# Chunked attention feeding a squared-ReLU FFN on one core: x of two groups transposed by DMA, and a block that begins in halves

## The chip, the core and the metric

The kernel runs on one core of one Trainium2 chip. The metric is the device time in microseconds (us), median of the runs. "PE" below is TensorE, "DVE" VectorE, "ACT" ScalarE, "POOL" GpSimd and "SP" SyncE, which here does nothing but issue DMAs.

## The reference

Attention over chunks of 64 tokens, for batch 8, 8 heads, 576 tokens and head size 64, and then an FFN without a gate:

```python
scores = scale * np.matmul(q_c, k_c.transpose(0, 1, 2, 4, 3))      # within a chunk of 64
attn = exp(scores - max); attn = attn / (attn.sum(-1) + 1e-09)
out = np.matmul(attn, v_c)
x = out.transpose(0, 2, 1, 3).reshape(B * S, H * D)                # 4608 x 512
h = np.maximum(x @ w_in, 0.0)                                      # 512 -> 2048
return h * h @ w_out                                               # 2048 -> 512
```

## The kernel before, in words

The 4608 tokens are 18 groups of 256 tokens; two groups make a block of 512, so there are nine blocks, numbered 0 to 8. For each group the kernel loads q, k and v, casts q and k to bf16 (`C`, lines L271 and L274; on POOL up to group 7, on ACT from group 8), transposes both (`TD`, L280, a DMA transpose on the SP queue from group 4), multiplies them (`SC`, scores, L303) and takes the exponential (L314, ACT), multiplies with v (`AV`, values, L330), divides by the sum (`rec` L337 and `x` L338, DVE), and transposes x (`XT`). In `XT`, groups below `FIRST_DMA_X` go through PE into PSUM and an ACT copy (L357, L361); the others use one DMA transpose (L351).

The FFN of a block has two phases. `ffn_in` goes over 16 d_ff tiles; each has four matmuls over d_model (L414) into one PSUM bank, a ReLU on ACT (`rl`, L430), and a square on DVE or ACT (`gT`, L442 or L440). `ffn_out` is a Strassen-like scheme (from block 1 on) with seven products, in this order: n (a22), m (a11), n (d5), m (d2), n (d1), m (d6), n (d7). Each product is 16 matmuls (L500) in two pieces. The differences d1 to d7 of quarters of gT are made on DVE (L395). The products named n share one PSUM bank, and those named m another; each sum is read out of its bank between two products, and the next product into that bank waits for the reading: n1 (L547, ACT), then nm = m + n1 (L457, DVE), n2 (L556, ACT), c21, s and c22 (L457, DVE), c11 (L583, ACT).

The order on each engine is written out by hand. Each generator yields after a piece of work, which is a slot: in block 2 before, `ffn_in` has slots 0 to 15 and `ffn_out` slots 16 to 29; in block 1 `ffn_in` has slots 0 to 31 and `ffn_out` slots 32 to 45. `at(slot, f, g)` puts the work `f` of group `g` after a slot, and `go_slots` lists the slots after which one more load is issued. While block j runs, its plan does SC, AV and XT for the groups of block j + 1 (`nxt`), and C and TD for those of block j + 2 (`far`). All of these emit their instructions at that place of every engine's queue: an instruction on DVE stands behind all that was emitted before it.

Scores and values share two PSUM tiles (`ps_att`, two buffers). One tile holds all scores of a group; values take one for each half of the group, and DVE's division gives it back. Block 1 is the first one whose `ffn_in` works in halves of its tokens: 256 columns at a time, two d_ff tiles to one PSUM bank (`pairs`).

Of the kernel before, what the change touches and what calls it, by code (L numbers as in the profile page):

```python
# [17 lines left out]
def kernel(  # L18
# [32 lines left out]
        return chunks[g][0][0] == chunks[g][3][0]  # L51

    FIRST_DMA_T = 4
    FIRST_DMA_X = 6
    SQUARES_ON_ACT = (10, 14, 3)
    SQUARES_ON_ACT_EARLY = (9, 10, 12, 7)
    BT = GT * max(len(b) for b in blocks)
# [103 lines left out]
    def go(pieces):  # L161
        for f in pieces:
            f()
# [180 lines left out]
    def transpose_x(g):  # L344
# [4 lines left out]
        dst = xTs[j][:, c // 128:c // 128 + 2].rearrange("p t h q -> p (t h) q")  # L349
        if g >= FIRST_DMA_X:  # L350
            nc.sync.dma_start_transpose(out=dst, in_=x.rearrange("p t h a d -> p (t h a d)"))  # L351
# [11 lines left out]
    C, TD = cast_qk, transpose_qk_dma  # L363
    SC, AV, XT = scores, values, transpose_x
# [18 lines left out]
    HF, HD, HT = n_ft // 2, d_model // 2, BT // 2  # L383
# [6 lines left out]
    def difference(j, name, part):  # L390
        if (name, j) not in state:
            state[name, j] = wst_pool.tile([128, 1024], FP32, name="w_st").bitcast(BF16).rearrange(
                "p (a f) -> p a f", a=HF)
        x, y = (quarters(j)[i][:, part] for i in DIFFERENCES[name])
        nc.vector.tensor_tensor(out=state[name, j][:, part], in0=x, in1=y, op=ALU.subtract)  # L395
# [4 lines left out]
    FT_EARLY = [ft + h for ft in range(N_EARLY) for h in (n_ft // 2, 0)]  # L400
    FT_EARLY += [ft for ft in FT_ORDER if ft not in FT_EARLY]

    def ffn_in(j, parts):
        if j not in gTs:
            gTs[j] = ffn_pool.tile([128, n_ft, BT], BF16, name="gT")
        gT, xT = gTs[j], xTs[j]

        pairs = j == 1
        for u, (c, n, fts, ft) in enumerate((*p, ft) for p in parts for ft in p[2]):
            second = pairs and u % 2  # L410
            if not second:
                h = ps_ffn.tile([128, 512], FP32, name="ps_ffn")
            for dt in range(n_dt):
                nc.tensor.matmul(  # L414
                    out=h[:, n:2 * n] if second else h[:, 0:n],
                    lhsT=w_in_bf[:, dt, ft * 128:(ft + 1) * 128],
                    rhs=xT[:, c // 128:(c + n) // 128, dt, :],
                    start=(dt == 0), stop=(dt == n_dt - 1))
            if pairs and not second:
                yield  # L420
                continue
            m = 2 * n if pairs else n
            if j < 3:
                if m == 512 or u % 2 == 0:
                    rl_tile = ffn_pool.tile([128, 512], FP32, name="rl", bufs=3).bitcast(BF16)
                rl = rl_tile[:, u % 2 * 512:] if m < 512 else rl_tile
            else:
                rl = ffn_pool.tile([128, 512], FP32, name="rl", bufs=3)
            rl = rl[:, 0:m]
            nc.scalar.activation(out=rl, in_=h[:, 0:m], func=AF.Relu)  # L430
            dst = gT[:, ft, c:c + n]
            if pairs:
                dst, rl = gT[:, ft - 1:ft + 1, c:c + n], rl.rearrange("p (a n) -> p a n", a=2)
                on_act = ft == 3 or (c > 0 and ft == 13)
            elif n == 512:
                on_act = ft in (SQUARES_ON_ACT_EARLY if fts is FT_EARLY else SQUARES_ON_ACT)
            else:
                on_act = True
            if on_act:
                nc.scalar.activation(out=dst, in_=rl, func=AF.Square)  # L440
            else:
                nc.vector.tensor_tensor(out=dst, in0=rl, in1=rl, op=ALU.mult)  # L442
            if fts is FT_EARLY and u == (11 if j == 2 else 8):

                for name in ("d5", "d2", "d1", "d6", "d7"):
                    difference(j, name, slice(0, N_EARLY))
            yield
# [11 lines left out]
    def sum_quarters(out, in0, in1, op=ALU.add, half=slice(None)):  # L459
        return lambda _: add(nc.vector, out[:, half], in0[:, half], in1[:, half], op)  # L460
# [163 lines left out]
    def pieces(grps):  # L624
        for g in grps:
            yield from qk_pieces(g)
        for g in grps:
            yield from v_pieces(g)


    first_ffn_in = ffn_in(0, [(0, HT, (0, 1)), (HT, HT, (0, 1)), (0, BT, range(2, n_ft))])

    go(pieces([0, 1]))
# [38 lines left out]
    for j, grps in enumerate(blocks):  # L672
        nxt = blocks[j + 1] if j + 1 < len(blocks) else []
        far = blocks[j + 2] if j + 2 < len(blocks) else []
        plan = {}

        def at(slot, f, g):
            plan.setdefault(slot, []).append((f, g))

        if j == 0:  # L680
            loads, go_slots = itertools.chain(*map(qk_pieces, far)), range(17)
            at(26, cast_last, None)
            at(28, sum_quarters(b11_p_b21, b11, b21), None)
            for slot, f in ((24, TA), (26, SC), (30, AV)):
                at(slot, f, nxt[0])
            at(33, XE, nxt[0])
            at(33, TQ, nxt[1])
            at(33, sum_quarters(b11_m_b22, b11, b22, ALU.subtract), None)
            phases = [first_ffn_in, ffn_out_by_ft(0)]
        elif j == 1:  # L690
            loads = itertools.chain(*map(v_pieces, nxt), *map(qk_pieces, far))
            go_slots = [*range(22, 25), *range(28, 48)]
            for slot, f in ((0, TK), (3, SC), (6, AV), (12, XT)):
                at(slot, f, grps[1])
            for i, g in enumerate(nxt):
                for slot, f in ((16 + 4 * i, C), (21 + 6 * i, TD), (37, SC), (39 + 2 * i, AV),
                                (42 + i, XT)):
                    at(slot, f, g)
            for i, g in enumerate(far):
                at(36 + 4 * i, C, g)  # L700
                at(42 + 3 * i, TD, g)
            at(2, sum_quarters(b11_p_b12, b11, b12), None)
            at(12, sum_quarters(b12_p_b22, b12, b22), None)
            at(20, sum_quarters(b21_p_b22, b21, b22), None)
            phases = [ffn_in(1, [(0, 256, FT_ORDER), (256, 256, FT_ORDER)]), ffn_out(1)]
        else:
            loads, go_slots = pieces(far), range(32)
            slots = {SC: (8, 8), AV: (11, 15), XT: (14, 18), C: (18, 20), TD: (20, 23)}
            if j == 3:
                go_slots = [*range(6), *range(13, 32)]  # L710
                slots.update({C: (18, 22), TD: (20, 24)})
            elif j > 3:

                go_slots = [*range(16 if j == len(blocks) - 4 else 6), *range(24, 32)]
            if j == 2:
                loads = itertools.chain(*map(v_pieces, nxt), loads)
                slots = {SC: (11, 11), AV: (13, 16), XT: (16, 19), C: (20, 23), TD: (22, 25)}
                go_slots = [*range(16), 23, 24, *range(26, 36)]
            for f in (SC, AV, XT):
                for i, g in enumerate(nxt):  # L720
                    at(slots[f][i], f, g)
            for f in (C, TD):
                for i, g in enumerate(far):
                    at(slots[f][i], f, g)
            phases = [ffn_in(j, [(0, BT, FT_EARLY)]), ffn_out(j)]
        slot = 0
        for phase in phases:
            for _ in phase:
                if slot in go_slots:
                    for f in loads:  # L730
                        f()
                        break
                for f, g in plan.get(slot, []):
                    f(g)
                slot += 1
        assert all(x < slot for x in plan), (j, slot, sorted(plan))
        go(loads)
# [30 lines left out]
```

## Time and profile before

| | |
|---|---|
| time, median of 3 runs | 280.07 us (279.8 to 280.27) |
| span of the profiled execution | 278.1 us |
| PE busy | 268.6 us (97%) |
| DVE busy | 182.3 us (66%) |
| ACT busy | 166.7 us (60%) |
| packets of the SP queue, share of 16 engines' span | 80.3% |

From 20 us on PE is busy almost without a break until the end (29.61 of the 30 us from 20 to 50, for one). The DMA engines are at nine tenths or more through most of the first 230 us, although PE rarely waits for them.

### The profile page before, as it was taken

What the parts mean: (1) busy time and instruction counts of PE and PEld (TensorE: products, weight loads), DVE (VectorE), ACT (ScalarE), POOL (GpSimd) and SP (SyncE); (2) the same over time, 40 slices, a digit from 0 to 9 for tenths busy, and PEclk for the clock granted to TensorE, in tenths of its full rate; (3) what the DMA queues carried; (4) which work ended last, traced back from release to release, by engine and by line L of the source; (5) the groups of instructions that cost most, each with busy time, mean ns of one, the idle gap of its engine ahead of it and who ended that gap; (6) DMA issues with size and microseconds to landing.
All of it is one profiled execution on the core that took longest, in us unless ns stands there. A gap on an engine that the chain in (4) does not pass through costs nothing.

```text
span 278.1 us, 7217 instructions
## 1 busy us (share of the span) xinstructions
PE 268.6 (97%) x2983; PEld 176.8 (64%) x2986; DVE 182.3 (66%) x317; ACT 166.7 (60%) x272; POOL 46.3 (17%) x78
## 2 busy tenths in 40 slices
PE   1999999999999999999999999999999999999995
PEld 1554444788874587448844874488448844874594
DVE  1255605776963795499549954995499549954883
ACT  1458704887348873977397819781978197319720
POOL 2037932242153000000000030003000300051000
PEclk9999999999999999999999999999999999999999
DMA  7999999999999999999999999769789960432003
GB/s 201 241 327 356 342 360 240 301 227 218 211 232 265 217 225 178 243 245 214 197 273 257 174 262 253 180 139 226 183 187 213 273 166 0 79 97 57 0 22 131
DMA packets 143088, 57.09 MB, mean 205 GB/s; under 512 B 110672, under 2 KB 140496, under 8 KB 143056
## 3 DMA queue, kind: packets, MB, share of 16 engines
q1 hardware_dynamic: 140784, 50.15, 80.3%
q0 software_dynamic: 1984, 6.29, 7.0%
q8 instruction: 23, 0.38, 0.6%
q10 hardware_dynamic: 288, 0.20, 0.2%
q14 instruction: 9, 0.07, 0.1%
HBM read 36.70 MB, written 9.44 MB: 166 GB/s over the span
## 4 chain that ended last, share of the span: by engine, by line
PE 93%; DVE 2%; DMA 2%; ACT 1%; issue 0%; SPq 0%
PE ps_ffn L414 45%; PE ps_ffn L500 34%; PE ps_ffn L601 4%; PE ps_att L303 2%; PE ps_att L330 2%; DMA k_sb<-in_k_dram 2%; PE ps_ffn L261 1%; PE ps_att L500 1%; PE ps_ffn L214 1%; DVE x L338 1%; PE ps_ffn L249 1%; PE ps_att L214 1%; ACT qkT L223 0%; ACT xT L361 0%; PE ps_att L357 0%
## 5 line engine op out<-in xcount | busy, mean ns | idle before, releaser
L414 PE MATMUL ps_ffn<-xT,w_in_bf 128*128 128x512 bf16 (+1 forms) x648 | 129.3, 356 | 0.1
L442 DVE TENSOR_TENSOR gT<-rl 128x512 bf16<-128x512 f32 (+1 forms) x108 | 67.3, 654 | 57.4 <-ACT rl L430 57.1
L414 PEld LDWEIGHTS <-w_in_bf 128*128 128x128 bf16 x648 | 61.7, 98 | 58.0 <-DMA xT<-x 0.3
L430 ACT ACTIVATE rl<-ps_ffn 128x512 f32<-128x512 f32 (+2 forms) x146 | 84.0, 590 | 21.6 <-PE ps_ffn L414 20.7
L500 PEld LDWEIGHTS <-w_st 128*128 128x128 bf16 x664 | 62.8, 98 | 7.1
L395 DVE TENSOR_TENSOR w_st<-gT 128x1536 bf16<-128x1536 bf16 (+2 forms) x75 | 50.3, 720 | 0.8 <-ACT gT L440 0.7
L500 PE MATMUL ps_ffn<-w_out_bf,w_st 128*128 128x256 bf16 x368 | 43.1, 273 | 0.0
L531 POOL DMA_DIRECT2D out_dram<-o_sb x16 | 11.4, 714 | 128.3 <-DVE o_sb L457 125.6
L500 PE MATMUL ps_ffn<-w_sum,w_st 128*128 128x256 bf16 x248 | 28.9, 273 | 0.1
L583 ACT COPY o_sb<-ps_ffn 128x512 f32<-128x512 f32 (+1 forms) x8 | 4.5, 558 | 37.9 <-PE ps_ffn L500 37.9
L500 PEld LDWEIGHTS <-gT 128*128 128x128 bf16 x264 | 24.7, 98 | 3.4
L338 DVE TENSOR_TENSOR x<-ps_att,rec 128x512 bf16<-128x512 f32 x36 | 24.9, 691 | 1.2
L440 ACT ACTIVATE gT<-rl 128x512 bf16<-128x512 f32 (+2 forms) x38 | 23.1, 607 | 1.2
L314 ACT ACTIVATE e<-ps_att 128x1024 bf16<-128x1024 f32 x18 | 17.6, 1024 | 5.7 <-PE ps_att L303 5.7
L500 PE MATMUL ps_ffn<-w_out_bf,gT 128*128 128x256 bf16 x128 | 15.3, 273 | 0.0
L500 PE MATMUL ps_ffn<-w_sum,gT 128*128 128x256 bf16 x120 | 14.6, 273 | 0.0
L601 PE MATMUL ps_ffn<-w_out_bf,gT 128*128 128x512 bf16 x61 | 14.2, 380 | 0.3 <-issue 0.2
L175 POOL CAST w_in_bf<-w_st 128x512 bf16<-128x512 f32 (+2 forms) x12 | 9.9, 842 | 18.2 <-DMA w_st<-in_moe_w_in_dram 18.2
L274 ACT CAST qkb<-k_sb 128x1024 bf16<-128x1024 f32 x10 | 10.5, 1046 | 1.5 <-DMA k_sb<-in_k_dram 1.5
L330 PEld LDWEIGHTS <-e 64*64 64x64 bf16 x576 | 6.5, 107 | 7.0 <-DVE gT L442 2.1
L271 ACT CAST qkb<-q_sb 128x1024 bf16<-128x1024 f32 x10 | 10.5, 1047 | 0.1
L601 PEld LDWEIGHTS <-gT 128*128 128x128 bf16 x64 | 6.0, 98 | 7.0
(59 smaller groups left out, 158.9 us busy)
## 6 DMA issues: line engine op xcount, KB each, us to landing
q_sb<-in_q_dram SPq DMA_DIRECT2D x16, 512.0 KB, 6.4
k_sb<-in_k_dram SPq DMA_DIRECT2D x24, 256.0 KB, 6.3
out_dram<-o_sb POOLq DMA_DIRECT2D x20, 256.0 KB, 4.4
ve_sb<-in_v_dram SPq DMA_DIRECT2D x32, 128.0 KB, 4.1
w_st<-in_moe_w_in_dram SPq DMA_DIRECT2D x8, 512.0 KB, 6.5
w_st<-in_moe_w_out_dram SPq DMA_DIRECT2D x8, 512.0 KB, 6.0
vo_sb<-in_v_dram SPq DMA_DIRECT2D x23, 128.0 KB, 3.9
out_dram<-o_sb SPq DMA_DIRECT2D x9, 256.0 KB, 2.8
```

What stands on the lines that cost most here:

```text
L271: copy(out=qkb[:, 0].rearrange("p (i h d) -> p i h d", i=2, h=H), in_=q_sb.rearrange("p (h i d) -> p i h d", h=H, i=2))
L314: nc.scalar.activation(out=e_out, in_=s_in, func=AF.Exp, scale=scale)
L330: nc.tensor.matmul(out=ps[64 * p:64 * p + 64, a, hp * (D + 1):(hp + 1) * (D + 1)], lhsT=e[64 * c:64 * c + 64, a, hp, t, :], rhs=vb[64 * c: ...
L338: nc.vector.tensor_tensor(out=x[:, t].rearrange("p h a d -> p a h d"), in0=o[:, :, :, 0:D], in1=rec.to_broadcast([128, 2, n_hp, D]), op=AL ...
L395: nc.vector.tensor_tensor(out=state[name, j][:, part], in0=x, in1=y, op=ALU.subtract)
L414: nc.tensor.matmul(out=h[:, n:2 * n] if second else h[:, 0:n], lhsT=w_in_bf[:, dt, ft * 128:(ft + 1) * 128], rhs=xT[:, c // 128:(c + n) // ...
L430: nc.scalar.activation(out=rl, in_=h[:, 0:m], func=AF.Relu)
L440: nc.scalar.activation(out=dst, in_=rl, func=AF.Square)
L442: nc.vector.tensor_tensor(out=dst, in0=rl, in1=rl, op=ALU.mult)
L500: nc.tensor.matmul(out=ps, lhsT=a[:, i, t * 128:(t + 1) * 128], rhs=b[:, i, c:c + n], start=(first and i == 0 and (last or k == 0)), stop= ...
L531: dma.dma_start(out=out[t0:t0 + HT, col:col + HD].rearrange("(t p) d -> p t d", p=128), in_=o_sb.rearrange("p (t d) -> p t d", d=HD))
L601: nc.tensor.matmul(out=o_ps[tt], lhsT=gT[:, ft, tt * 128:(tt + 1) * 128], rhs=w_out_bf[:, ft, :], start=(ft == 0), stop=(ft == n_ft - 1))
```

## The change

x of groups 4 and 5, which make block 2, is to be transposed by DMA as that of the later groups is, so that PE and ACT are spared these transposes. A DMA takes longer to arrive than a PE transpose, and the two are needed right at the start of block 2. So block 2 begins with four d_ff tiles (8, 9, 0, 1) for the first half of its tokens (group 4) and then for the second half (group 5), before it goes on with the other twelve over all 512 tokens; `ffn_in` of block 2 thus has 20 slots, the first eight of which are half as long. To let the two transposes come early in the SP queue, the load of q and k of group 7 and the transposes of q and k of groups 6 and 7 move to the end of block 1 and into block 2, and so the scores, values and x transposes of groups 6 and 7 move to later slots of block 2.

```diff
-    FIRST_DMA_X = 6
+    FIRST_DMA_X = 4
...
-        pairs = j == 1
-        for u, (c, n, fts, ft) in enumerate((*p, ft) for p in parts for ft in p[2]):
+        for u, (c, n, _, ft) in enumerate((*p, ft) for p in parts for ft in p[2]):
+            pairs = j > 0 and n < 512
...
-                on_act = ft == 3 or (c > 0 and ft == 13)
+                on_act = ft == 3 or (c > 0 and ft == (13 if j == 1 else 9))
             elif n == 512:
-                on_act = ft in (SQUARES_ON_ACT_EARLY if fts is FT_EARLY else SQUARES_ON_ACT)
+                on_act = ft in (SQUARES_ON_ACT_EARLY if j > 1 else SQUARES_ON_ACT)
...
-            if fts is FT_EARLY and u == (11 if j == 2 else 8):
+            if j > 1 and u == (15 if j == 2 else 8):
...
-            go_slots = [*range(22, 25), *range(28, 48)]
+            go_slots = [*range(22, 25), *range(28, 37), 43, 44]
...
-            for i, g in enumerate(far):
-                at(36 + 4 * i, C, g)
-                at(42 + 3 * i, TD, g)
+            at(36, C, far[0])
...
-                slots = {SC: (11, 11), AV: (13, 16), XT: (16, 19), C: (20, 23), TD: (22, 25)}
-                go_slots = [*range(16), 23, 24, *range(26, 36)]
+                slots = {SC: (18, 18), AV: (20, 23), XT: (23, 26), C: (24, 27), TD: (26, 29)}
+                go_slots = [*range(20), 27, 28, *range(30, 40)]
+                for slot, f, g in ((0, TD, nxt[0]), (0, C, nxt[1]), (8, TD, nxt[1])):
+                    at(slot, f, g)
...
-            phases = [ffn_in(j, [(0, BT, FT_EARLY)]), ffn_out(j)]
+            parts = [(0, BT, FT_EARLY)]
+            if j == 2:
+
+                both = [8, 9, 0, 1]
+                parts = [(0, HT, both), (HT, HT, both),
+                         (0, BT, [ft for ft in FT_EARLY if ft not in both])]
+            phases = [ffn_in(j, parts), ffn_out(j)]
```

## The prediction

> **What bounds the kernel now.** I read the page first (busy times, then the chain), then the chain in order of time around the change, then the table of stretches, then the timelines of DVE and ACT at the end of block 2.
>
> ```profile
> PE 268.6 (97%) x2983; PEld 176.8 (64%) x2986; DVE 182.3 (66%) x317; ACT 166.7 (60%) x272; POOL 46.3 (17%) x78
> PE 93%; DVE 2%; DMA 2%; ACT 1%; issue 0%; SPq 0%
> ...
> 78.31 0.48 PE ps_att L357 x8
> 78.79 0.87 PE ps_ffn L500 x8
> 79.66 0.45 PE ps_att L357 x8
> 80.11 1.75 PE ps_ffn L500 x16
> 81.86 10.36 PE ps_ffn L414 x48
> ...
> 98.18 11.46 PE ps_ffn L500 x104
> ...
> 67.00:82.00 15.00, 14.94 (x257) 12.80 (x255) 12.88 (x20) 5.56 (x8) 3.59 (x4) 1.00 1.05 234
> 82.00:97.00 15.00, 15.00 (x163) 7.09 (x162) 7.39 (x19) 12.54 (x22) 3.32 (x5) 1.00 0.98 228
> 97.00:110.00 13.00, 13.00 (x146) 11.11 (x144) 10.41 (x17) 6.75 (x9) 0.00 (x0) 1.00 1.16 197
> ```
>
> The reader is to see that PE sets the end. In the three stretches around the change (their first numbers after the length are PE, PEld, DVE, ACT) PE idles 0.06 us in 43. So at most what is taken off PE can be won, and any new wait on PE is lost in full. The chain shows what goes: the two L357 entries, 0.48 + 0.45 = 0.93 us. The third stretch has DVE at 10.41 of 13.00 us: `ffn_out` of block 2 is where DVE is nearly full. How its queue stands there:
>
> ```profile
> 97.72 0.41 DVE L442 TENSOR_TENSOR gT<-rl 128x512 bf16<-128x512 bf16 x1
> 98.24 1.83 DVE L395 TENSOR_TENSOR w_st<-gT 128x1536 bf16<-128x1536 bf16 x2
> 99.98 0.20 DVE L337 RECIPROCAL rec<-ps_att 128x8 f32<-128x8 f32 x1
> 100.22 0.69 DVE L338 TENSOR_TENSOR x<-ps_att,rec 128x512 bf16<-128x512 f32 x1
> 100.83 0.20 DVE L337 RECIPROCAL rec<-ps_att 128x8 f32<-128x8 f32 x1
> 101.06 0.69 DVE L338 TENSOR_TENSOR x<-ps_att,rec 128x512 bf16<-128x512 f32 x1
> 101.67 0.68 DVE L457 TENSOR_TENSOR nm<-ps_ffn,n 128x512 f32<-128x512 f32 x1
> ```
>
> Here d5 and d2 (1.74 us from start to next start) are followed by x of group 7 (1.69 us) and by nm, which ends at 102.36. nm reads bank m, and product d2 writes it next. By the chain d2 begins at 98.18 + 0.87 + 1.75 + 1.75 = 102.55. Before, nm has 0.19 us to spare.
>
> [...] nm stands behind x of group 7 though it needs nothing of it. [...] here 16 of 256 take 1.75 us (109 ns each) and 48 of 512 take 10.36 us (216 ns)[...]. [...] so I use issue to landing. [...] Here an xT transpose takes 3.4 us issued at 103.15, and 5.5 us issued at 128.78 behind loads.
>
> **The change part by part.**
>
> *1. PE transposes of groups 4 and 5 go:* -0.93 us on PE. Not all of it comes home. The last product of block 1 (n, d7) needs bank n read by s, which DVE does after x of group 5, at 78.87 with 0.68 us, so until 79.55. Without transposes PE is there at 80.11 - 0.93 = 79.18. It waits until 79.6, so block 2 begins at 79.6 + 1.75 = 81.4 instead of 81.86: a gain of 0.48 us. ACT's two L361 copies (1.01 us each) go too, but ACT is idle there (5.56 of 15 us).
>
> *2. xT of group 4.* x is done at 76.63 and SP, with the load of q of group 7 put behind, is free: issued 76.7, landed 3.4 later (the unclogged case), 80.1. It is in time for 81.4: nothing.
>
> *3. xT of group 5.* x is done at 78.95. Ahead in the queue is the 512 KB of q of group 7, issued about 78.0. An unclogged q took 4.3 us to land (issued at 71.10), so 82.3, and the transpose about 1.0 us more (that of 128.78 landed 0.96 after the load ahead): 83.3, or up to 84.0 with a 256 KB store between. PE needs it after 16 half matmuls, 81.4 + 1.75 = 83.15. A wait between 0 and 0.9 us; I take 0.3.
>
> *4. Halves.* 16 matmuls of 512 become 32 of 256[...].
>
> *5. qT and kT of group 7* now come after the nine v loads and after q and k of group 7, whose casts run on an idle POOL. From 77.80 (k of group 6 landed) until it lands the queue moves: two xT of 1.0, q 1.8, k 1.7, four stores of about 0.7, nine v in 4.1 (91.41 to 95.55 before), and two qkT of 1.8; about 16 us, plus 1 us idle at the start: 94.9, give or take 1.2. The scores at slot 18 need it at 81.4 + 0.3 + 8 x 0.437 + 11 x 0.866 + 0.32 = 95.0. Before, it landed at 91.0 for 92.2. A wait between 0 and 1.2; I take 0.2.
>
> *6. Attention of groups 6 and 7 later.* Let P be the end of block 2's `ffn_in` on PE: 96.91 before. The amount of work is the same, but x of group 6 (DVE, 1.69 us), which lay at 96.03 to 97.72 inside `ffn_in`, where DVE has 7.39 of 15 us, now stands behind d5 and d2 in the full `ffn_out`, with x of group 7 behind it and nm behind both. The exponentials, too, now come just ahead of the last ReLU and its square on ACT. ACT's timeline shows their price:
>
> ```profile
> 92.25 0.60 ACT L430 ACTIVATE rl<-ps_ffn 128x512 bf16<-128x512 f32 x1 [0.27 <-PE ps_ffn L414]
> 92.75 1.94 ACT L314 ACTIVATE e<-ps_att 128x1024 bf16<-128x1024 f32 x2
> 94.55 1.11 ACT L430 ACTIVATE rl<-ps_ffn 128x512 bf16<-128x512 f32 x2
> ```
>
> Scores began at 92.22 and the next ReLU at 94.55, 2.33 us later. In the changed order scores begin 0.64 + 0.87 = 1.51 us ahead of P; so the last ReLU starts at P + 0.82, its square ends 0.63 + 0.63 later at P + 2.08, and d5 starts at P + 2.11 (before: 98.24 = P + 1.33). Then:
> - d5 and d2 to P + 3.85; x of group 6 gives back its first `ps_att` tile at P + 4.78 (0.24 + 0.69), the second at P + 5.63.
> - PE: n's first piece 0.87, values of group 6 0.40, second piece 0.87, m 1.75: P + 3.89. Values of group 7 need those two tiles: PE waits 0.9, runs 0.2, waits 0.6, runs 0.2: P + 5.85. Behind them stands all of PE's queue.
> - d5 product until P + 7.60. nm on DVE: P + 3.85 + 2 x 1.69 = 7.23, ends P + 7.92. Product d2 waits another 0.36.
> Sum: 1.9 us. Product d1 then comes at P + 9.7, when its difference (nm + 0.6 + 0.9 = P + 8.7) is there; afterwards nothing new. If ACT were not late, d5 would start at P + 1.33 and the wait would be 1.1; with the square 0.3 later it is 2.2. These are its ends.
>
> *7. After that.* x of group 7 is ready at P + 7.2, and block 3 begins at about P + 15: its transpose (5.1 us clogged) is hidden, and later blocks follow unchanged.
>
> Sum: -0.48 + 0.05 + 0.3 + 0.2 + 1.9 = +1.97 us, 280.07 -> 282.0 us.
>
> **The rivals.**
> - *The gain stays (other side).* If DVE's queue did not hold PE, the time would be 280.07 - 0.48 = 279.6, or 279.14 if even s in block 1 gave no wait. For it: x transposes and attention do the same work on all engines, DVE at 66%. Against: the 0.19 us of slack at nm against 1.69 us put ahead of it. 7%.
> - *Nearly no change.* The `ffn_out` wait shrinks to about 0.5 us, as though the ACT delay were absent and DVE's steps overlapped more, and transfers are in time: 280.07 - 0.48 + 0.05 + 0.5 = 280.1. 5%.
> - *The transfers wait too.* xT of group 5 at its bad end (0.9) and qkT of group 7 at its bad end (1.2) on top of part 6: -0.48 + 0.05 + 0.9 + 1.2 + 1.9 = +3.6, 283.6. For it: the DMA share is 1.00 or so throughout. Against: before, loads landed ahead of PE. 18%.
>
> **How the numbers follow.** My forecast has 70%, the rivals 7, 5 and 18. The predicted time is the forecast's, 282.0. The range: low from the small end of part 6 (1.1) with a transfer wait of 0.2, +0.9, 280.9; high from the last rival, 283.6. Faster by over 0.2% (0.56 us) needs the full gain: 0.07; within: 0.05; slower: 0.88.
>
> **What would show it.** In the changed profile: the L357 entries after 75 us gone; block 2 starting near 81.4; PE waiting at L330 for DVE x, about 1.5 us, and at L500 for nm, about 0.4, within the first 8 us of block 2's `ffn_out`; DVE without idle from d5 to d6 there; block 2 ending near 111.6 instead of 109.64, and blocks 3 to 8 as long as before. I am wrong if PE runs through the start of block 2's `ffn_out` without these waits, or if the larger wait is for xT or qkT.

## The result, and the profile after

| | before | after |
|---|---|---|
| time, median | 280.11 us, beside the runs of after | 286.66 us (286.18 to 287.93, 4 runs) |
| ratio | | 1.0245, 95% interval 1.0215 to 1.0274 |
| span of the profiled execution | 278.1 us | 286.1 us |
| block 2's `ffn_in` begins on PE | 81.69 | 81.28 |
| block 2's `ffn_out` begins | 96.75 | 102.49 |
| block 3 begins | 109.64 | 117.52 |

The change makes the kernel 6.6 us slower. Slower was forecast, but by 2.0 us, and the time lies outside the range. (The profiled execution of after is the slowest of its four, so its span shows 1.3 us more than the median does.) Every ratio in this document compares a version with runs of the kernel before taken beside it and leaves out the few runs in a slower state (over 1.5% above the fastest of the same kernel), so it need not be the quotient of the medians. The page of after: busy times, the slices of PE and of its granted clock, and the group of the `ffn_in` matmuls, whose last column is the idle time ahead of them:

```profile
PE 270.3 (94%) x2986; PEld 178.3 (62%) x2986; DVE 181.7 (63%) x317; ACT 164.5 (57%) x270; POOL 46.8 (16%) x78
...
PE   2989999999958998999999999999999999999995
...
PEclk9999999999995999999999999999999999999999
...
L414 PE MATMUL ps_ffn<-xT,w_in_bf 128*128 128x512 bf16 (+1 forms) x664 | 132.1, 357 | 4.2 <-DMA xT<-x 3.6
```

PE is busy for 1.7 us more although the change takes work off it, most of its new idle time is in one place, and the clock has a dip there. The table of stretches of after (PE first, then PEld, DVE, ACT, POOL, the granted clock, DMA share, GB/s) and PE's timeline show that place:

```profile
67.00:82.00 15.00, 14.51 (x245) 12.40 (x243) 12.81 (x20) 3.88 (x6) 4.17 (x5) 1.00 0.87 174
82.00:97.00 15.00, 11.37 (x54) 6.08 (x53) 2.77 (x6) 7.27 (x14) 2.80 (x3) 0.77 1.05 247
```

```profile
79.53 1.91 PE L500 MATMUL ps_ffn<-w_out_bf,w_st 128*128 128x256 bf16 x16 [0.42 <-DVE n L457]
81.28 1.91 PE L414 MATMUL ps_ffn<-xT,w_in_bf 128*128 128x256 bf16 x16
86.82 5.73 PE L414 MATMUL ps_ffn<-xT,w_in_bf 128*128 128x256 bf16 x21 [3.63 <-DMA xT<-x]
```

The first half of block 2 runs at once. The second half waits 3.63 us for xT of group 5, which was issued at 79.67 and landed at 86.77. SP's timeline of after has its issue, with xT of group 4 and q of group 7 ahead of it and the k loads of group 7 behind it:

```profile
76.71 2.23 SPq L351 DMA_TRANSPOSE xT<-x  x1
79.03 0.53 SPq L106 DMA_DIRECT2D q_sb<-in_q_dram  x1
79.67 2.80 SPq L351 DMA_TRANSPOSE xT<-x  x1
82.56 2.82 SPq L120 DMA_DIRECT2D k_sb<-in_k_dram  x2
```

And 2.6 us after PE had run out of work the granted clock fell to 0.5 for 6.83 us (clock 0.77 in the second stretch): the 60 `ffn_in` matmuls before the scores took 14.15 us, against 11.35 for the same ones at full clock in a later experiment (the changed kernel without the stores, below).

The rest of the way is the start of block 2's `ffn_out`. PE's and then DVE's timeline of after:

```profile
107.42 0.22 PE L330 MATMUL ps_att<-ve_sb,e 64*64 64x65 bf16 x2 [0.77 <-DVE x L338]
...
108.26 0.22 PE L330 MATMUL ps_att<-ve_sb,e 64*64 64x65 bf16 x2 [0.51 <-DVE x L338]
```

```profile
104.69 1.83 DVE L395 TENSOR_TENSOR w_st<-gT 128x1536 bf16<-128x1536 bf16 x2 [2.46 <-ACT gT L440]
...
109.80 0.68 DVE L457 TENSOR_TENSOR nm<-ps_ffn,n 128x512 f32<-128x512 f32 x1
```

These are the forecast waits, at the forecast places. `ffn_out` of block 2 takes 117.52 - 102.49 = 15.03 us, before 12.89; it now holds one more set of values (0.40), so the waits cost 1.7.

Sum to the start of block 3: block 2 begins 0.41 earlier, 3.63 of waiting, 14.15 - 11.35 = 2.80 for the clock, 1.7 in `ffn_out`: +7.7 of the +7.88 that the table shows. This is the path of one execution. The clock's part is not the same in all: the five executions on record had a mean clock of 0.988 (the profiled one), 0.994, 0.992, 0.994 and 1.000, and the last, which is not in the median, took 287.21 us all the same.

Why did one transpose take 7.1 us? The profile offers a difference on a queue that the prediction had hardly looked at, that of POOL, which issues the four stores of block 1's output (L531). Its timeline before, and then after:

```profile
78.91 0.71 POOL L531 DMA_DIRECT2D out_dram<-o_sb  x1
81.15 1.04 POOL L271 CAST qkb<-q_sb 128x1024 bf16<-128x1024 f32 x1 [1.53 <-DMA q_sb<-in_q_dram]
82.74 1.04 POOL L274 CAST qkb<-k_sb 128x1024 bf16<-128x1024 f32 x1 [0.54 <-DMA k_sb<-in_k_dram]
83.72 2.14 POOL L531 DMA_DIRECT2D out_dram<-o_sb  x3
```

```profile
79.24 0.71 POOL L531 DMA_DIRECT2D out_dram<-o_sb  x1
80.37 1.43 POOL L531 DMA_DIRECT2D out_dram<-o_sb  x2 [0.42 <-DVE o_sb L457]
82.36 0.72 POOL L531 DMA_DIRECT2D out_dram<-o_sb  x1 [0.55 <-ACT o_sb L583]
84.52 1.03 POOL L271 CAST qkb<-q_sb 128x1024 bf16<-128x1024 f32 x1 [1.44 <-DMA q_sb<-in_q_dram]
```

Before, the casts of group 7 stood between the first store and the other three. After, those casts come later, and all four stores leave between 79.24 and 83.08, while xT of group 5 is in flight.

### The profile page after: what moved, and what is told of

Same layout as the page of the kernel before. It is cut to its first block, busy times and chain, and to the rows that moved or that the text cites. A ratio compares the mean times of both kernels' runs of the same rounds, so it can differ in the third digit from the quotient of the medians.

```text
span 286.1 us, 7227 instructions
## 1 busy us (share of the span) xinstructions
PE 270.3 (94%) x2986; PEld 178.3 (62%) x2986; DVE 181.7 (63%) x317; ACT 164.5 (57%) x270; POOL 46.8 (16%) x78
## 4 chain that ended last, share of the span: by engine, by line
PE 60%; DVE 0%; issue 0%
PE ps_ffn L414 29%; PE ps_ffn L500 27%; PE ps_att L330 1%; PE ps_att L500 1%; PE ps_att L303 1%; DVE o_sb L589 0%
## 5 line engine op out<-in xcount | busy, mean ns | idle before, releaser
L414 PE MATMUL ps_ffn<-xT,w_in_bf 128*128 128x512 bf16 (+1 forms) x664 | 132.1, 357 | 4.2 <-DMA xT<-x 3.6
L442 DVE TENSOR_TENSOR gT<-rl 128x512 bf16<-128x512 f32 (+1 forms) x108 | 66.6, 646 | 63.1 <-ACT rl L430 62.7
L414 PEld LDWEIGHTS <-w_in_bf 128*128 128x128 bf16 x664 | 64.5, 99 | 62.6 <-DMA xT<-x 3.9
L531 POOL DMA_DIRECT2D out_dram<-o_sb x16 | 11.4, 715 | 131.4 <-DVE o_sb L457 128.1
L314 ACT ACTIVATE e<-ps_att 128x1024 bf16<-128x1024 f32 x18 | 17.6, 1024 | 5.7 <-PE ps_att L303 5.7
```

The lines of the kernel that those rows point to most:

```text
L314: nc.scalar.activation(out=e_out, in_=s_in, func=AF.Exp, scale=scale)
L414: nc.tensor.matmul(out=h[:, n:2 * n] if second else h[:, 0:n], lhsT=w_in_bf[:, dt, ft * 128:(ft + 1) * 128], rhs=xT[:, c // 128:(c + n) // ...
L531: dma.dma_start(out=out[t0:t0 + HT, col:col + HD].rearrange("(t p) d -> p t d", p=128), in_=o_sb.rearrange("p (t d) -> p t d", d=HD))
```

## The experiments

What is disputed is why the transposes came late: the loads around them and the order of the SP queue, or the stores. The expectations say which theory forecasts what. "Idle" is PE's idle time in block 2 and at the start of block 3 by its timeline. Waits and landings are those of the one execution that was profiled, which is not always near the median.

### Undoing single parts

**Later attention alone.** The kernel before, with only the attention of groups 6 and 7 moved to later slots of block 2 (its `ffn_in` has 16 slots here):

```diff
-                slots = {SC: (11, 11), AV: (13, 16), XT: (16, 19), C: (20, 23), TD: (22, 25)}
+                slots = {SC: (14, 14), AV: (16, 19), XT: (19, 22), C: (20, 23), TD: (22, 25)}
```

> The kernel before with one edit: in block 2 scores, values and x transposes of groups 6 and 7 come three d_ff tiles later, at the places they have in the changed kernel (slots 14, 16 and 19, 19 and 22). All transfers are in time then, so this is the price of the later attention alone. Theory P6: PE waits about 0.9 and 0.6 us at values of group 7 and 0.4 us at product d2, together 1.9: 282.0 us (281.6 to 282.4). Rival: DVE and ACT have room, and it is within 0.2 us of 280.1.

Measured: 281.44 us, ratio 1.0025 (1.0007 to 1.0044), so +0.2 to +1.2 us; in the profile block 2 takes 1.6 more. PE's timeline has the very gaps of after:

```profile
101.11 0.22 PE L330 MATMUL ps_att<-ve_sb,e 64*64 64x65 bf16 x2 [0.77 <-DVE x L338]
...
101.95 0.22 PE L330 MATMUL ps_att<-ve_sb,e 64*64 64x65 bf16 x2 [0.51 <-DVE x L338]
```

So step 6 of the prediction is there by itself. It was forecast at 1.9 us; the profile has less, the runs have less still, and the larger loss is elsewhere.

**x on PE again.** The changed kernel with the x of groups 4 and 5 transposed by PE:

```diff
-    FIRST_DMA_X = 4
+    FIRST_DMA_X = 6
```

> The changed kernel with x of groups 4 and 5 transposed on PE as before, all else as changed (halves, later loads and transposes, later attention of groups 6 and 7). Theory: what is left is the wait on DVE in ffn_out, 1.9 us, the halves 0.05 and possibly a wait for the transposes of q and k of group 7 up to 1: 282.1 us (281.7 to 283). Rival: the halves or the later attention cost nothing and all of the loss is the transposes' arrival: 280.1. Rival: the loss lies in the later loads: about 285.

Measured: 283.01 us (281.69 to 287.13, 13 runs), ratio 1.0093 (1.0063 to 1.0123). The wait for xT is gone, but PE waits 3.28 us at the scores (L303) for qkT of group 7, landed at 98.83; qkT of group 6 had taken 11.0 us (82.16 to 93.15). A transpose is long here too, and it is another one. (The profiled execution took 285.84 us, with a clock of 0.993. In 8 of the 13 runs the mean clock was 0.998 or more, so these waits need not be those of a typical run.)

**xT of group 5 ahead of q of group 7 in the queue.**

```diff
-            go_slots = [*range(22, 25), *range(28, 37), 43, 44]
+            go_slots = [*range(22, 25), *range(28, 37), 44, 45]
```

> One edit to the changed kernel: the load of q of group 7 comes one slot later, so that the x transpose of group 5 stands ahead of it in the SP queue. Theory Q (it was late because 512 KB of q stood ahead of it): it lands at about 82.5 to 83.2 instead of 86.8, PE waits at most 0.2 us for it, the clock stays at full, and what is left is the wait on DVE in ffn_out (1.9), the gain of 0.5 and nothing else: 281.6 us (281.2 to 282.2). Theory S (it was late because block 1's output stores shared the DMA engines): the stores are still there, it lands after 85 and the time stays above 284. Theory X (a DMA transpose on a busy queue takes some 7 us whatever stands around it): about 286.

Measured: 287.81 us, ratio 1.0259 (1.0211 to 1.0307): a miss, for 281.6 was expected. The landing came as theory Q said: xT of group 5 took 3.9 us and was there at 82.86, in time, with all four stores still on POOL. So the stores alone did not make it late; it took them and q of group 7 ahead of it. PE's timeline shows the price at the scores, where the wait for qkT of group 7 (forecast to land at 94.9) had been hidden in after:

```profile
100.14 0.64 PE L303 MATMUL ps_att<-qkT 64*64 64x64 bf16 x32 [5.26 <-DMA qkT<-qkb]
```

**PE kept busy in the wait.** Some 3.6 us of matmuls on the identity matrix, whose result nobody reads, stand between the two halves:

```diff
+            if j == 2 and u == 4:
+                keep_busy(64)
```

> One edit to the changed kernel: 16 matmuls of 512 columns on the identity (3.45 us), whose result nobody reads, between the first and the second half of block 2's first four d_ff tiles, where PE waits for the x transpose of group 5. If the fall of the clock was caused by PE's idleness and cost 2.8 us, the matmuls of block 2 stay at full speed and the time is about 283.8 us. If the clock did not matter, it stays at 286.7. If the transpose is in truth not what PE waits for, the filler adds 3.4: 290.

Measured: 286.77 us, ratio 1.0208 (1.0172 to 1.0244). The clock stays at 1.0, as forecast, but the time does not come down to the forecast 283.8. Most of the gain is taken back by the next wait in line:

```profile
87.03 11.42 PE L416 MATMUL ps_ffn<-xT,w_in_bf 128*128 128x256 bf16 x60 [0.29 <-DMA xT<-x]
...
100.23 0.45 PE L303 MATMUL ps_att<-qkT 64*64 64x64 bf16 x32 [1.40 <-DMA qkT<-qkb]
```

What follows: the clock's fall made `ffn_in` 2.8 us longer, but to take it away alone gained 0.0037 in the ratio, about 1 us, which the intervals do not tell from nothing, for behind it stood qkT of group 7, and behind that xT of group 7. From about 77 to 115 us the transfers are late as a row, and mending one shows the next.

### The order of the SP queue

**qkT of group 7 ahead of the v loads**, on top of xT of group 5 ahead of q of group 7:

```diff
-                for slot, f, g in ((0, TD, nxt[0]), (0, C, nxt[1]), (8, TD, nxt[1])):
+                for slot, f, g in ((0, TD, nxt[0]), (0, C, nxt[1]), (2, TD, nxt[1])):
```

> Two edits to the changed kernel: the load of q of group 7 comes one slot later, behind the x transpose of group 5 (as in the run where this alone left PE waiting 5.3 us for qkT of group 7), and the transpose of q and k of group 7 is issued at slot 2 of block 2 instead of slot 8, so ahead of six of the nine v loads. Theory T (after xT is in time, the wait on PE is for qkT of group 7, and it is late because of its place in the SP queue): it lands at 95.5 to 96.5 instead of 100.1, PE waits about 1 to 1.5 us at the scores with no fall of the clock, and the wait on DVE in ffn_out comes back to about 1.9: 283.3 us (282.5 to 284.3). Rival L (it is late because the loads of q and k of group 7 and the casts are): it lands at 98 or later, above 285.

Measured: 286.20 us, ratio 1.0198 (1.0138 to 1.0258), against an expected 283.3. Idle 1.51 for qkT of group 7 (96.24), and now 2.76 for xT of group 7 (114.86).

**As that, with the loads for block 4 behind xT of group 7:**

```diff
-                go_slots = [*range(20), 27, 28, *range(30, 40)]
+                go_slots = [*range(16), 27, 28, *range(30, 40)]
```

> As the run with qkT of group 7 at slot 2 (xT of group 7 landed at 114.86 there and PE waited 2.76 us for it at the start of block 3), and the loads of block 2 stop after slot 15, so that four v loads of group 8 come behind the x transposes of groups 6 and 7, as in the kernel before. Theory K (the SP queue is the bound from 77 to 115 us, and PE's wait moves to the next thing it needs from the queue whenever one is removed): xT of group 7 lands 2.5 us earlier, about 112.3, PE waits 0 to 0.5 us for it, and the time falls by that much, 283.6 us (283 to 284.6). Rival: xT of group 7 is late because of the division of group 7 on DVE or because of its own duration; it stays near 114.9 and the time near 286.2.

Measured: 284.21 us, ratio 1.0114 (1.0081 to 1.0148): idle 1.52 for qkT and 0.86 for xT of group 7. The best order of the queue with all the transfers in it, and still 1% over the kernel before.

**The loads of group 7 never held back:** in after, `go_slots` of block 1 end with `range(28, 40)`, and qkT of group 7 is put to slot 2.

> The changed kernel with the loads of q and k of group 7 back at slots 37 to 39 of block 1, ahead of both x transposes, and qkT of group 7 at slot 2 of block 2. The queue then is not held for 3 us by the wait for x of group 4. Theory K: xT of group 4 lands late, at about 84, and PE waits 2.5 to 3 us at the start of block 2, but not for qkT of group 7 (landed by 94); xT of group 7 lands at about 112 instead of 114.7. Sum: 283.7 us (282.8 to 284.8). Rival (the held queue does not matter; late arrivals come from transposes being slow): xT of group 7 near 115 all the same, 286 or more.

Measured: 289.34 us, ratio 1.0281 (1.0231 to 1.0331). In the profiled execution (291.25 us, the slowest of the four) PE waits 4.62 us for xT of group 4 and 1.12 for that of group 5, and the mean clock is 0.982. That holding loads back was what cost the time is refuted.

**The same with x on PE** (`FIRST_DMA_X = 6`):

> As the run before it, but x of groups 4 and 5 transposed on PE: what is left of the change is the halves, the later place of the two qkT and the later attention of groups 6 and 7. Theory K with the measured price of the later attention (1.4 us): no wait for any transfer, 280.1 + 1.4 + 0.05 = 281.5 us (281.1 to 282.2), 1.5 us under the same kernel with the loads held back. Rival: the later qkT costs by itself; PE waits for it, above 282.5.

Measured: 285.46 us, ratio 1.0151 (1.0079 to 1.0224). The four runs lie far apart: 282.89 and 284.04 us with the clock at 1.000, 286.88 and 286.93 with 0.994. The order of the loads is close to the kernel before, but in the profile, which is of the slowest, qkT of group 6 takes 11.2 us (6.7 there), and xT of group 7 comes 3.00 us late. While the stores landed (until 92.08), packets took long: from 84 to 89 us one of the stores' 4096 bytes took 0.25 to 0.49 us on the mean of each microsecond, and one of 256 bytes up to 0.12; at other times 0.16 and 0.018.

### The stores moved

**The four stores held until slot 10 of block 2, still on POOL:** in `ffn_out` of block 1 each `store(...)` is put on a list.

```diff
+                at(10, lambda _: go(held), None)
```

> One edit to the changed kernel: the four output stores of block 1 are issued at slot 10 of block 2 instead of at the end of block 1; q of group 7 stays ahead of the x transpose of group 5. Theory Q: the landing moves little (86), PE still waits about 3 us, above 285. Theory S: the transpose's packets end about 1 us earlier[...]: it lands at about 84.4 to 84.8, PE waits 1.3 to 1.7 us[...], and the time is about 283 to 283.5. Theory X: 286.

Measured: 284.69 us, ratio 1.0141 (1.0103 to 1.0179). xT of group 5 takes 5.0 us instead of 7.1, PE waits 0.92 for it, the clock stays at 1.0; qkT of group 7 (98.03) is waited for, 1.94.

**The four stores on the SP queue behind qkT of group 7** (with the first two edits of the queue's order):

> As the run before it, and block 1's four output stores are issued on the SP queue at slot 10 of block 2, behind all transposes of that time. Theory T with theory S (the stores shared the DMA engines with the loads and transposes of that time): qkT of group 7 lands by 94, PE waits neither for xT nor for qkT, and what is left is the gain of 0.5 and the wait of 1.9 on DVE in ffn_out: 281.6 us (281.2 to 282.2). Rival: the stores do not matter to qkT; same time as the run before it.

Measured: 286.03 us, ratio 1.0189 (1.0136 to 1.0241). No wait for xT of group 5 nor for qkT of group 7, which took about 4 us. But everything behind the stores is later: 1.67 us at product d1 (L502 in this kernel, by way of n2 on ACT, which stood behind a cast of group 8 that waited for its load) and 2.76 for xT of group 7.

**As that, with the scores and values of groups 6 and 7 spread:**

```diff
-                slots = {SC: (18, 18), AV: (20, 23), XT: (23, 26), C: (24, 27), TD: (26, 29)}
+                slots = {SC: (15, 18), AV: (17, 21), XT: (20, 24), C: (24, 27), TD: (26, 29)}
```

> As the run before it, and the attention of groups 6 and 7 is pulled apart: scores at slots 15 and 18, values at 17 and 21, x transposes at 20 and 24 (all of it 18, 20 and 23, 23 and 26 before). The division of group 6 lies inside ffn_in again, and only one exponential is ahead of the last ReLU. Theory P6 (the wait in ffn_out comes from two divisions ahead of nm on DVE): the wait shrinks to 0.3 or less, and the time is about 279.8 us (279.4 to 280.4), at or a little under the kernel before. Rival: the wait in ffn_out stays at 1.9, 281.6.

Measured: 286.65 us, ratio 1.0213 (1.0149 to 1.0277). The waits of step 6 are gone, but PE waits for v of group 6 (0.62 and 0.25), for n2 (2.07) and for xT of group 7 (0.36).

**The four stores on POOL behind the casts of group 7**, where three of them stood before: `at(1, lambda _: go(held), None)`, once on top of the best order of the queue, once on top of that and with SC 15 and 18, AV 18 and 21, XT 20 and 24 and qkT of group 7 at slot 4 instead of 2, and once with x on PE and the loads never held back.

> As the run with xT of group 5 ahead of q of group 7, qkT of group 7 at slot 2 and four v loads behind xT of group 7 (284.2 us), with block 1's output stores on POOL behind the casts of group 7. Theory S2: qkT of group 6 lands in 6 us or less instead of 7.4, qkT of group 7 by 95, xT of group 7 by 111.5; PE waits for transfers at most 0.5 us in all; what is left is the gain of 0.4 and the later attention, 1.4: 281.3 us (280.9 to 282.2). Rival: no change, 284.2.

> As the run before it, and the attention of groups 6 and 7 pulled apart (scores at slots 15 and 18, values at 18 and 21, x transposes at 20 and 24; qkT of group 7 at slot 4). If the waits at values of group 7 and at product d2 come from two divisions in a row ahead of nm, they fall from 1.4 us to 0.3 or less, and the time is about 280.2 us (279.7 to 281), the same as the kernel before. Rival: a new wait takes their place, above 281.

> As the run with x on PE and the queue never held (285.5 us, where qkT of group 6 took 11.2 us to land and PE waited 3.0 us for xT of group 7), with one edit: block 1's four output stores are issued on POOL behind the casts of group 7, not ahead of them. Theory S2 (stores and DMA transposes in flight together slow each other; in the kernel before three of the stores stood behind those casts and so came after qkT of group 6): qkT of group 6 lands in 7 us or less, xT of group 7 before block 3 needs it, and only the later attention is left: 281.5 us (281.1 to 282.4). Rival (the later place of the qkT is what makes the queue late): 284 or more.

Measured: 286.25 us, ratio 1.0169 (1.0123 to 1.0215); 286.62, 1.0213 (1.0176 to 1.0251); 284.13, 1.0113 (1.0051 to 1.0175). In the first and third qkT of group 6 drops to 6.3 and 5.7 us, and qkT of group 7 becomes the long one: 9.3 and 9.5 us; PE waits 3.50 us for it in the first and 0.94 for xT of group 7 in the third. In the second PE waits 2.39 at the scores and 1.00 for the exponential.

What follows from these: what shares its time with the stores, or stands behind them, is mostly late (xT of group 5 ahead of q of group 7, at 3.9 us, was not). Moving them chooses another victim. Of the versions so far that move transfers or stores, only the best order of the queue took about the time that was expected of it (283.6 us). The others were expected at 279.8 to 283.7 us and measured 284.13 to 289.34: most removed the wait that they were made for and met another.

### The stores left out

> The changed kernel with the four output stores of block 1 left out (block 1's output is not written); the arithmetic is all there. S2 (a DMA transpose in flight beside those stores is stretched): xT of group 5, 7.1 us in the changed kernel, takes 4.5 to 5.5, PE waits for it at most 1.5, the clock stays at 1.0, but qkT of group 7 is still issued late (96.3) and lands by 100, so a wait for it of 1 to 3 us appears; total 283 to 285.5. S1 (the transpose is long because q of group 7 and the v loads lie around it): xT of group 5 still 6.5 to 7.5, wait 3 or more, clock falls, 286 to 287.

> s1_v8_behind_xT7 with the four stores of block 1 left out (block 1's output is not written). S2: qkT of group 6 about 5.5, qkT of group 7 lands by 95, no wait at the scores, xT of group 7 by 111.5; only the gaps of step 6 (about 1.3) stay: 281 to 282.5. S1: qkT of group 7 still lands at about 96.4 with a wait of 1.5: 284.

> s3_x_on_PE_queue_never_held with the four stores of block 1 left out (block 1's output is not written). S2: qkT of group 6 about 5.7 us instead of 11.2, xT of group 7 lands by 111.5, wait for it under 0.5: 281.5 to 283. S1: qkT of group 6 over 9 us, wait of 3 for xT of group 7, 285.5.

> The kernel before with the four stores of block 1 left out (block 1's output is not written). Control. Both: PE has no wait to give back there, so 279.5 to 280.2, same as before. S2 adds: qkT of group 6 no shorter by over 1 us than before, since three of the four stores were behind the casts of group 7 and missed it.

The edit is the same in all four. Block 1's output is then not written; the arithmetic is all there:

```diff
         def store(dma, o_sb, half, col, t):
+            if j == 1:
+                return
```

| version | with the stores of block 1, ratio | without, ratio | without, us |
|---|---|---|---|
| changed kernel | 1.0245 (1.0215 to 1.0274) | 1.0088 (1.0057 to 1.0118) | 282.50 |
| best order of the queue | 1.0114 (1.0081 to 1.0148) | 1.0071 (1.0048 to 1.0094) | 282.14 |
| x on PE, loads never held back | 1.0151 (1.0079 to 1.0224) | 1.0059 (1.0034 to 1.0083) | 281.72 |
| kernel before | 1 | 0.9989 (0.9973 to 1.0004) | 279.85 |

The same 1 MB of stores costs the kernel before nothing that can be measured, and the changed kernel 1.6%, 4.2 us between the medians. Whether another 1 MB left out, of loads for instance, would have given as much was not tried. The transfer view, asked for the instant of issue of one transpose, gives its time to landing (us, last column): xT of group 5 in after, then without the stores.

```profile
xT<-x SPq DMA_TRANSPOSE x1, 7.1
```

```profile
xT<-x SPq DMA_TRANSPOSE x1, 4.7
```

And qkT of group 7 in the kernel before, then without the stores:

```profile
qkT<-qkb SPq DMA_TRANSPOSE x1, 7.2
```

```profile
qkT<-qkb SPq DMA_TRANSPOSE x1, 3.8
```

The third and fourth line are the answer to why before did not suffer. The stores stretched a transpose there as well, by 3.4 us (qkT of group 6, expected to be missed by them, goes from 6.7 to 5.2, though in two other versions without stores it took 6.3 and 6.4). But it landed at 91.04 and was needed at 92.22. In after the stretched one is xT of group 5, behind q of group 7 and with no slack at all. PE's timeline of the changed kernel without the stores:

```profile
79.75 1.91 PE L500 MATMUL ps_ffn<-w_out_bf,w_st 128*128 128x256 bf16 x16 [0.42 <-DVE n L457]
...
83.88 11.42 PE L414 MATMUL ps_ffn<-xT,w_in_bf 128*128 128x256 bf16 x60 [0.47 <-DMA xT<-x]
...
101.67 0.22 PE L330 MATMUL ps_att<-ve_sb,e 64*64 64x65 bf16 x2 [0.61 <-DVE x L338]
...
102.51 0.22 PE L330 MATMUL ps_att<-ve_sb,e 64*64 64x65 bf16 x2 [0.51 <-DVE x L338]
...
112.10 6.22 PE L414 MATMUL ps_ffn<-xT,w_in_bf 128*128 128x512 bf16 x28 [0.17 <-DMA xT<-x]
```

All waits here but the last are the prediction's, near their size, and the last, 0.17 us for xT of group 7, is small; the clock does not fall (mean 0.998), and qkT of group 7 lands at 95.60. The best order of the queue no longer waits at the scores, and with x on PE qkT of group 6 takes 4.2 us instead of 11.2. In all three the waits of step 6 remain, 1.1 to 1.3 us at the values by PE's timeline, against the 1.7 to 2.5 us (0.6 to 0.9%) that stay.

How the stores stretch a transpose, the packets tell in part. The four stores are 256 packets of 4096 bytes, and at 0.16 us each that is 41 us of one DMA engine, 2.6 us of all sixteen; xT of group 5 was 2.4 longer. In the trace of after, packets of both queues run side by side until 85.1, when the last of the 1024 packets of xT of group 5 (256 bytes each, found by counting) begins: 5.4 us after the issue. In the 1.67 us from there to the landing 171 of the stores' packets of 4096 bytes ran, and 36 of 256 bytes. Without the stores the same packet begins 4.0 us after the issue and the landing follows 0.68 later. So 1.4 of the 2.4 us lie ahead of the last packet and 1.0 behind it. By what the stores lengthen either part was not shown, and why no packet of the k loads, whose issue began at 82.56, ran between 85.1 and 86.2 is open. And the 7 us by which qkT of group 6 grew in the version with x on PE are more than the stores' 2.6; there the packets themselves were slower, and why is left open. No version with all its work in it beat the kernel before.

## Why the prediction was wrong, by its steps

- *1, transposes off PE:* right. The wait for DVE's reading of bank n is there (0.42), and block 2 begins 0.41 earlier (0.07 of it is there by 73.8 us, ahead of the change); forecast 0.48.
- *2, xT of group 4:* right: issued 76.71, landed 80.31, so 3.60 us, where the two L357 entries in the chain of before are 0.48 and 0.45; forecast 80.1.
- *3, xT of group 5: the step that failed.* It allowed a wait of 0 to 0.9 and took 0.3; it was 3.63. The mis-sized term is the landing, "83.3, or up to 84.0 with a 256 KB store between". It let one store pass, following the SP queue alone; all four passed, from POOL, while it was in flight. The landing at 86.77 is 3.47 later than 83.3. Of this, 1.03 is the issue of q of group 7 at 79.03 instead of 78.0: xT of group 4 ahead of it held SP for 2.23 us, and that was before the first store. 0.70 is q itself, 5.00 us instead of 4.3, and 1.74 is the transpose, which landed 2.74 behind q instead of 1.0. Without the stores q took 4.33 and the transpose landed 0.97 behind it, at 83.83, so by this comparison the last two terms, 2.4 us in all, are the stores', and the forecast's own figures for the unclogged case were right. That the later casts move the stores forward on POOL could be read from the POOL timeline and the order of that engine, and was not.
- *A term that was missing:* the sum had none for the clock. In the profiled execution a wait of 3.63 made the matmuls behind it 2.80 us longer. (Taken away alone, the fall gained little, as shown above: qkT of group 7 stood behind it.) The rival with late transfers, too, had only waits in it, so even its 283.6 was too low.
- *4, halves:* no sign of more than the 0.05 forecast. The chain of before gives the same as an estimate: 16 matmuls of 256 in 1.75 us and 48 of 512 in 10.36 are 109.4 and 215.8 ns each, so a pair of halves costs 2.9 ns more than a whole, and sixteen pairs 0.05 us.
- *5, qkT of group 7:* forecast to land at 94.9, landed at 100.24. It cost nothing in after, where the scores came at 100.97, because xT of group 5 had made everything late. The first cause mended, it cost 5.26. The term of the four stores (0.7 each) was in this sum, but not that SP's own issues took longer beside the stores: 2.82 us for the two k loads, 1.44 without the stores.
- *6, later attention:* right in mechanism, place and nearly size. d5 was forecast 2.11 us after the end of `ffn_in` and started 2.03 after it (its last matmul ends at 102.66); nm was forecast to end 7.92 after it and ended 7.82 after. The waits were 0.77, 0.51 and 0.10 by PE's idle time, 1.7 by the length of the phase; forecast 1.9. Alone, this part costs 0.2 to 1.2 us by the runs' times.
- *7, nothing later:* true of after, where block 3 was late enough. With the earlier waits mended, xT of group 7 was waited for (0.86 to 2.76 us in three versions with x by DMA), so the step held only by the failure of step 3.

The forecast of 2.0 us is about what the change costs where the stores are away: 282.50 against 279.85, 2.65 us. The other 4 us go when the stores go. In the profile they are the stretched transpose without slack and the fall of the clock that its wait brought, with the late qkT of group 7 right behind.

## What to carry to other kernels

Before moving a transfer up to where an engine waits for it, list everything that all issuers will have in flight at that time, plain output stores included, and add their packets' time to its landing (here 2.6 us of packets, by the estimate above, and 2.4 us more for xT of group 5; with x on PE qkT of group 6 grew by 7); an issuer whose other work is delayed may send its stores earlier than before. Look at the slack of each transfer, not only at waits: a stretched transfer is invisible until a change takes its slack away (qkT of group 7 in the kernel before: 7.2 us, and no wait). When transfers run as a late row, mending one wait shows the next, so leave a suspect out altogether instead of moving it.

## What the runs showed of the hardware

- In after the granted clock stood at half for 6.83 us, from 85.76 to 92.58; its record has 75.09 us at full clock before that and 194.56 behind it. PE had stopped at 83.19, 2.6 us before the fall, so most of the loss lay behind the wait: PE worked for 5.76 of the 6.83 us.
- The mean clock of the profiled execution goes with the longest wait of PE that its timeline shows in block 2 and at the start of block 3, but not by its length alone. The eight with a mean of 0.982 to 0.994 had longest waits of 2.07 us (stores behind qkT of group 7 with the attention spread, 0.993), 2.39 (stores behind the casts with the attention spread, 0.994), 3.00 (x on PE, loads never held back, 0.994), 3.28 (x on PE, 0.993), 3.50 (stores behind the casts, 0.988), 3.63 (after, 0.988), 4.62 (loads never held back, 0.982) and 5.26 (xT of group 5 ahead of q of group 7, 0.992). Of the twelve with 0.998 or more, ten had none over 1.94 (stores at slot 10 of block 2), and two had one of 2.76 (qkT of group 7 ahead of the v loads; stores behind qkT of group 7). What decides between a wait of 2.07 us with a fall and one of 2.76 without was not shown. With PE kept busy in the wait of after the mean was 1.000.
- A DMA transpose that shared its time with four 256 KB stores took 7.1, 7.2 and 11.2 us where it took 4.7, 3.8 and 4.2 with the stores left out, though they come from another queue (xT of group 5 in after, qkT of group 7 in before, qkT of group 6 with x on PE and the loads never held back). Ahead of the loads of its own queue one took 3.9 us beside them.
- With stores and transposes in flight together, packets slowed in some traces: with x on PE those of 256 bytes rose from 0.018 to as much as 0.12 us and those of 4096 from 0.16 to as much as 0.49, on the mean of a microsecond. In before the mean of the stores' packets was 0.18 us and the longest 0.50. In after they kept to 0.16.
